# A third pair of expert weight buffers, earlier dispatch and reads of two batches, and a re-dealt attention order, in an attention kernel that feeds a mixture of experts

## The chip, the cores and the metric

The kernel runs on one core of one Trainium2 chip. The metric is the time of one execution in microseconds (us), as the device measures it; of several runs the median is quoted. A core has a matrix engine (PE; its weight loads are shown apart as PEld), a vector engine (DVE), a scalar engine (ACT), a general engine (POOL) and a sequencer that only issues transfers (SP). Each runs its own instructions in order and waits on semaphores for the others. Transfers run on 16 DMA engines. In this kernel those issued from SP (q, k, v, reads of the lists, transposing reads) form one queue, and those issued from POOL (weights with a cast to 16 bits, row scatters) another.

## The reference

Attention with a relative position bias (8 batches, 8 heads, 576 positions, head size 64), and then a routed pair of matrix products: each of the 4608 tokens goes to one of 8 experts by a hash of its id.

```python
scores = scale * q @ k.T + bias_table[bucket(i - j)]
attn = exp(scores - max); attn /= attn.sum()
x = (attn @ v)                       # reshaped to (4608, 512)
expert_idx = token_ids * 2654435761 % 8
for e in range(8):
    xe = x[expert_idx == e]
    out[expert_idx == e] = relu(xe @ w1[e]) @ w2[e]     # w1: 512 x 1024, w2: 1024 x 512
```

## The kernel before, in words

The work has two stages, whose instructions are written out by hand in the order in which each engine takes them.

**Attention.** It goes over 32 pairs (n): batch b = n // 4, heads 2m and 2m+1 with m = n % 4. A pair has five steps g. In each, PE forms score products into a PSUM tile `ps` (L528, bias through L505), ACT takes the exponential into `att` (L570) and, later, PE multiplies `att` with the values into `px` (L638). These value products trail the scores by more than a pair: a generator cuts them into 45 portions for each pair (9 for each of the five query tiles), and `advance(av, ...)` deals out a number of portions after each step, from the table `SHARE` (even pairs, odd pairs). DVE divides `px` into `x_all` (L648), applies a correction factor to `att` (L580) and moves transposed q and k out of PSUM into `kq` (L441). POOL casts q and k to 16 bits (L248). ACT is paced by 160 exponentials.

**Routing.** From the token ids, `route()` computes for each token its row in its expert's list of 640 rows. It is a generator as well; one piece is taken at steps 0 and 2 of pairs 6 to 9. DVE does nearly all of it (`oh`, `inc`, `rnk`, `rank`, `odd`, `ds2`).

**Dispatch.** `x_all` is a ring of 6 batches. When a batch is done, its five tiles join the list `waiting`, and `send` scatters them into the lists in HBM (`t_xperm`, L663, POOL), 2, 2 and 1 a pair from pair 10 on. `gather_head` reads the first 384 rows of the lists of experts 0 and 1 (`xpn`, L158, SP) once the scatters of batches 0 to 5, and 0 to 6, have landed; it stands at pairs 28 and 31. The first rows of expert 0 are transposed on PE in pair 31 (L848), and its first layer runs among the last value products (L862).

**Experts.** The parts are: experts 0 and 1, early rows; experts 0 and 1, last rows; experts 2 to 7 with 640 rows each. The first layer (`hps`, L1097 or L1117) needs `w1t`, the second (`ops`, L1149) `w2t`. DVE copies results to `ok` (L1154, 8 buffers), POOL scatters them to the output (L1157). There are two buffers of each weight. After the first layer of expert e, `load_w1(e + 2)` (L145) goes into the buffer just freed; after its second layer `load_w2(e + 2)` (L151). Experts 2 to 7 read their rows through transposing transfers issued on SP (`xpt`, L1042), into four buffers, so that the fifth and sixth wait for the first layers of experts 2 and 3.

A last stage, under a condition that does not hold for this input, recomputes everything in a general way (`fb`); it is not executed here.

## Time and profile before

| | us |
|---|---|
| median of 3 runs | 359.07 |
| lowest, highest | 352.07, 371.37 |
| the profiled execution | 347.01 |
| its span, first to last instruction | 345.2 |
| mean granted TensorE clock in it | 0.976 of full |
| busy: PE, ACT, DVE, POOL | 307.3, 202.4, 162.6, 155.2 |

The profiled execution is a run of its own, and it was shorter than the three timed ones. The span is 1.8 us below its time. Shares over the whole span mix two stages: attention up to about 180 us, where PE and ACT are both full, and the experts after it, where ACT and DVE have little to do.

### The profile page before, as it was taken

To read this page: it belongs to the slowest core of one execution; us is meant where nothing else is said; L and a number is where in the kernel's file an instruction comes from. 1 tells how busy PE (TensorE), PEld (TensorE's weight loads), DVE (VectorE), ACT (ScalarE), POOL (GpSimd) and SP (SyncE) were. 2 spreads that over 40 slices of the span, in tenths; PEclk is the share of its full clock that TensorE was granted. 3 is DMA by queue.
4 is the path that set the end of the run, shared out by engine and by line. 5 is a ranking of instruction groups with operands and counts; after the bars stand their busy time and mean duration, and the time that the engine had idled before them with its cause. 6 is when DMAs were issued, how large, how long until landed. Compare 5 with 4: busy or idle time off the path is not lost.

```text
span 345.2 us, 8717 instructions
## 1 busy us (share of the span) xinstructions
PE 307.3 (89%) x3595; PEld 194.0 (56%) x3595; DVE 162.6 (47%) x385; ACT 202.4 (59%) x239; POOL 155.2 (45%) x206
## 2 busy tenths in 40 slices
PE   7688898999999999999899995199997699899991
PEld 3356565676666677666665562164744346464651
DVE  3436899887879788887433311003021040312121
ACT  3799988999999999999831122050503306041410
POOL 5466742475677666566144245004204333253232
PEclk9999999999999999999999999589999899999998
DMA  6998998969899978998936999999999999997212
GB/s 171 252 259 253 296 273 247 297 177 297 243 261 273 262 210 259 208 155 132 234 98 156 216 187 100 224 229 84 83 221 159 219 170 215 229 214 177 86 65 89
DMA packets 102435, 68.86 MB, mean 199 GB/s; under 512 B 28001, under 2 KB 93929, under 8 KB 102386
## 3 DMA queue, kind: packets, MB, share of 16 engines
q1 hardware_dynamic: 84048, 36.66, 49.4%
q0 software_dynamic: 18080, 31.48, 44.5%
q8 instruction: 30, 0.49, 0.6%
q14 instruction: 19, 0.16, 0.2%
q10 hardware_dynamic: 258, 0.07, 0.1%
HBM read 65.24 MB, written 17.36 MB: 239 GB/s over the span
## 4 chain that ended last, share of the span: by engine, by line
PE 41%; DMA 28%; issue 10%; DVE 8%; ACT 6%; POOL 4%; SPq 1%; POOLq 0%; ACTq 0%; DVEq 0%
PE px L638 9%; PE ops L1149 8%; DMA w2t<-in_moe_w_dram 7%; DMA out_dram<-ok,ids 7%; PE ps L528 7%; DMA w1t<-in_moe_w_dram 6%; ACT att L570 6%; PE hps L1097 5%; PE ps L505 5%; DMA xpn<-t_xperm 3%; PE pqk L435 3%; POOL out_dram L1157 3%; DVE att L580 2%; DMA btr<-t_g 2%; PE hps L862 2%
## 5 line engine op out<-in xcount | busy, mean ns | idle before, releaser
L570 ACT ACTIVATE att<-ps 128x1024 f16<-128x1024 f32 x160 | 150.4, 1057 | 10.8 <-PE ps L528 8.8
L1154 DVE COPY ok<-ops 128x512 f32<-128x512 f32 (+1 forms) x41 | 27.8, 678 | 127.1 <-PE ops L1149 119.8
L1103 ACT ACTIVATE h<-hps 128x640 f16<-128x640 f32 x48 | 33.7, 703 | 86.6 <-PE hps L1097 86.6
L1149 PE MATMUL ops<-w2t,h 128*128 128x512 f16 (+1 forms) x328 | 73.3, 380 | 5.8 <-DMA w2t<-in_moe_w_dram 4.6
L1157 POOL DMA_INDIRECT out_dram<-ok,ids x40 | 39.9, 997 | 68.0 <-DVE ok L1154 36.5
L1097 PE MATMUL hps<-xpt,w1t 128*128 128x320 f16 x384 | 54.9, 305 | 12.7 <-DMA w1t<-in_moe_w_dram 12.7
L638 PEld LDWEIGHTS <-att 128*128 128x128 f16 x1408 | 54.7, 97 | 12.4 <-issue 7.5
L638 PE MATMUL px<-va,att 128*128 128x65 f16 x1280 | 59.4, 193 | 0.5 <-DVE xpt L853 0.3
L1149 PEld LDWEIGHTS <-h 128*128 128x128 f16 x328 | 32.0, 99 | 43.1 <-DMA w2t<-in_moe_w_dram 5.2
L1097 PEld LDWEIGHTS <-w1t 128*128 128x128 f16 x384 | 38.1, 100 | 29.8 <-DMA w1t<-in_moe_w_dram 13.7
L663 POOL DMA_INDIRECT t_xperm<-x_all,ds x40 | 41.6, 1040 | 21.9 <-DVE x_all L648 13.9
L505 PE MATMUL ps<-btb,idents 128*128 128x384 f16 (+1 forms) x256 | 45.2, 261 | 0.6 <-DMA btb<-t_f 0.3
L528 PE MATMUL ps<-kq 64*128 64x512 f16 x256 | 42.5, 382 | 2.0 <-DVE kq L441 1.2
L580 DVE TENSOR_TENSOR att<-att,ebd 128x768 f16<-128x768 f16 x64 | 42.3, 678 | 4.0 <-ACT ebd L603 4.0
L248 POOL CAST kh<-kf 128x512 f16<-128x512 f32 x31 | 19.7, 637 | 51.6 <-PE pqk L435 26.1
L648 DVE TENSOR_TENSOR x_all<-px,rcp 128x384 f16<-128x384 f32 x64 | 31.4, 491 | 2.2
L441 DVE COPY kq<-pqk 128x1024 f16<-128x1024 f16 x31 | 21.4, 690 | 19.9 <-PE pqk L435 19.7
L505 PEld LDWEIGHTS <-idents 128*128 128x128 f16 x336 | 20.9, 97 | 17.4 <-issue 16.0
L528 PEld LDWEIGHTS <-kq 64*128 64x128 f16 x512 | 14.9, 94 | 20.6 <-issue 13.1
L145 POOL DMA_DIRECT2D w1t<-in_moe_w_dram x8 | 6.5, 808 | 38.4 <-PE hps L1097 24.2
L248 POOL CAST qh<-qf 128x512 f16<-128x512 f32 x30 | 19.1, 637 | 3.5 <-DMA qf<-in_q_dram 3.4
L1125 ACT ACTIVATE h<-hps 128x768 f16<-128x768 f32 (+1 forms) x8 | 7.3, 916 | 22.4 <-PE hps L1117 22.4
(110 smaller groups left out, 274.4 us busy)
## 6 DMA issues: line engine op xcount, KB each, us to landing
w1t<-in_moe_w_dram POOLq DMA_DIRECT2D x8, 1024.0 KB, 23.6
w2t<-in_moe_w_dram POOLq DMA_DIRECT2D x8, 1024.0 KB, 18.9
vf<-in_v_dram SPq DMA_DIRECT2D x28, 256.0 KB
kf<-in_k_dram SPq DMA_DIRECT2D x26, 256.0 KB
qf<-in_q_dram SPq DMA_DIRECT2D x26, 256.0 KB
t_xperm<-zx SPq DMA_DIRECT2D x8, 192.8 KB
kf<-in_k_dram SPq DMA_DIRECT2D x12, 128.0 KB
qf<-in_q_dram SPq DMA_DIRECT2D x12, 128.0 KB
```

Of the source, the lines that this page charges most:

```text
L248: (eng or nc.gpsimd).tensor_copy(out=dst[n][:, :, :, :].transpose([0, 2, 1, 3]), in_=src[n // 2][:, 2 * (n % 2) : 2 * (n % 2) + 2].rearran ...
L505: nc.tensor.matmul(out=out, lhsT=idents[:, which, :], rhs=rhs, start=start, stop=True, skip_group_check=True,)
L528: nc.tensor.matmul(out=ps[:, hh, o : o + rhs.shape[1]], lhsT=lhsT, rhs=rhs, start=not biased and (g < KT or t == 0), stop=True, skip_group ...
L570: nc.scalar.activation(out=att[:, g, :, :], in_=ps[:, :, :], func=AF.Exp, bias=0.0, scale=scale,)
L580: nc.vector.tensor_tensor(out=a, in0=a, in1=ebd[:, 2 * m : 2 * m + 2, 1 - c : 3 - c, :], op=ALU.mult,)
L638: nc.tensor.matmul(out=po, lhsT=lhsT, rhs=rhs, start=(i == 0), stop=(i == len(todo) - 1), skip_group_check=True,)
L648: nc.vector.tensor_tensor(out=x_all[:, b % NRING, its[0] : its[0] + ni, :DM].rearrange("p t (m h d) -> p t m h d", h=2, m=NPAIR)[:, :, m, ...
L663: sc_in = nc.gpsimd.indirect_dma_start(out=xperm_d.ap()[:, :], out_offset=bass.IndirectOffsetOnAxis(ap=ds2[:, NIT * b + t : NIT * b + t + ...
L1097: nc.tensor.matmul(out=hps[:, nr, : n // 2], lhsT=w[:, kt, ts(ft, P)], rhs=xt[i][:, kt, ts(nr, n // 2)], start=(kt == 0), stop=(kt == NPT ...
L1103: nc.scalar.activation(out=hs[i][:, ft, :].rearrange("p (r n) -> p r n", r=2), in_=hps[:, :, : n // 2], func=AF.Relu, bias=0.0, scale=1.0,)
L1149: nc.tensor.matmul(out=ops[:, :w], lhsT=hs[i][:, ft, ts(sc, P)], rhs=w2t[e % 2][:, ft, d0 : d0 + w], start=(ft == 0), stop=(ft == NFT - 1),)
L1157: so = nc.gpsimd.indirect_dma_start(out=out[:, :], out_offset=bass.IndirectOffsetOnAxis(ap=ids[i][:, sc, :], axis=0), in_=ok[:, :], in_off ...
```

## The change

- **Weights**: three buffers of each weight (`NW = 3`) where there were two. The loads for experts 0, 1 and 2 all stand in the attention: w1 and w2 of expert 0 at pairs 22 and 24 (before: 24 and 26), of expert 1 at pairs 27 and 28 (28 and 30), of expert 2 in pairs 30 and 31 (before: in the expert stage). In the expert stage each load is for expert e + 3.
- **Dispatch**: sending starts at pair 14, with 2 or 3 tiles a pair; batches 5 and 6 are sent within one pair as soon as they are done; `gather_head` stands right behind them, at pairs 26 and 30. The ring `x_all` has 4 batches.
- **Value products**: portions dealt 9, 9, 9, 0, 18 in even pairs and 9, 9, 0, 9, 18 in odd ones (before: 18, 9, 9, 0, 18 and 9, 9, 0, 9, 9), with their own deals for pairs 2, 3 and 5.
- **Ramp**: the transposes of pair 2, the load of the last rows of k, the transposes of batch 1's last rows and the spread of its keys stand at other steps of pairs 0 to 3.
- **Routing**: its pieces are taken in pairs 8, 9, 12 and 13, its loads in pairs 5 and 6.
- `ok` has 14 buffers. The stage that is not executed is cut in two halves.

```diff
-    NRING = 6
+    NRING = 4
+    NW = 3
...
-            out=w1t[e % 2][:, k0:k1, :],
+            out=w1t[e % NW][:, k0:k1, :],
...
-        load_rest(0, "kq")
+        load_rest(0, "q")
...
         load_band(0, 2, nc.sync)
+        load_rest(0, "k")
...
-        SHARE = ((18, 9, 9, 0, 18), (9, 9, 0, 9, 9))
+        SHARE = ((9, 9, 9, 0, 18), (9, 9, 0, 9, 18))
+        DEAL = {2: (18, 18, 9, 9, 9), 3: (18, 0, 9, 9, 9), 5: (18, 0, 0, 9, 18)}
...
-            if n >= 10:
-                send((2, 2, 1)[(n - 10) % 3])
-            if n == NP - 4:
-                gather_head(0)
-            if n == NP - 1:
-                gather_head(1)
+            if 14 <= n < 25:
+                send(3 if n % 3 == 0 else 2)
...
-            if n >= 24 and n % 2 == 0:
-                (load_w1 if n % 4 == 0 else load_w2)((n - 24) // 4)
+            if n in (22, 24):
+                (load_w1 if n == 22 else load_w2)(0)
+            if n in (27, 28):
+                (load_w1 if n == 27 else load_w2)(1)
...
-            if 6 <= n < 10 and g in (0, 2):
+            if n in (8, 9, 12, 13) and g in (0, 2):
                 next(routing, None)
...
-                if b == B - 1:
-                    send(2)
+            if (m, g) in ((1, 2), (1, 4), (2, 0)) and b >= B - 2:
+                send(2)
+            if (m, g) == (2, 1) and b >= B - 2:
+                assert not waiting
+                gather_head(b - B + 2)
+            if (b, m, g) in ((B - 1, 2, 3), (B - 1, 3, 1)):
+                (load_w1 if m == 2 else load_w2)(2)
...
-            ok = mo.tile([P, DM], F32, name="ok", bufs=8)
+            ok = mo.tile([P, DM], F32, name="ok", bufs=14)
...
-            after = e + 2 if c1 == NSC and e + 2 < E else None
+            after = e + NW if c1 == NSC and e + NW < E else None
```

POOL's row, before, from pair 28 of the attention into the expert stage (each `w1t_N` and `w2t_N` is one buffer, `x_all` the rows of a batch, `ok` a tile of results):

```order
L145 DMA w1t_69<-in_moe_w_dram 128x4x1024
L663 DMA t_xperm<-x_all,ds_59 9728x514 x3
L151 DMA w2t_71<-in_moe_w_dram 128x8x512
L663 DMA t_xperm<-x_all,ds_59 9728x514 x7
L1157 DMA out_dram<-ok,ids 4608x512 x6
L145 DMA w1t_68<-in_moe_w_dram 128x4x1024
L1157 DMA out_dram<-ok,ids 4608x512 x2
L151 DMA w2t_70<-in_moe_w_dram 128x8x512
L145 DMA w1t_69<-in_moe_w_dram 128x4x1024
L1157 DMA out_dram<-ok,ids 4608x512 x2
L151 DMA w2t_71<-in_moe_w_dram 128x8x512
L145 DMA w1t_68<-in_moe_w_dram 128x4x1024
```

The same place after the change, from pair 28 on:

```order
L152 DMA w2t_72<-in_moe_w_dram 128x8x512
L664 DMA t_xperm<-x_all,ds_59 9728x514 x5
L146 DMA w1t_70<-in_moe_w_dram 128x4x1024
L152 DMA w2t_73<-in_moe_w_dram 128x8x512
L664 DMA t_xperm<-x_all,ds_59 9728x514 x5
L1166 DMA out_dram<-ok,ids 4608x512 x6
L146 DMA w1t_68<-in_moe_w_dram 128x4x1024
L1166 DMA out_dram<-ok,ids 4608x512 x2
L152 DMA w2t_71<-in_moe_w_dram 128x8x512
L146 DMA w1t_69<-in_moe_w_dram 128x4x1024
```

The two loads into the third buffers (`w1t_70`, `w2t_73`) now stand ahead of the last batch's five scatters; the first load behind the six result scatters is now for expert 3, where it was for expert 2.

DVE's row, before, in pair 7, around one piece of the routing (`inc`, `rnk`) among the correction of `att`, the division of `px` and the spread of a batch's last keys and queries (`kzr`, `qtr`):

```order
L580 TENSOR_TENSOR att<-att,ebd 128x4x192
L342 SCALAR_TENSOR_TENSOR inc<-keep,rps 128x320
L348 TENSOR_TENSOR rnk<-inc,rps 128x320
L462 COPY kzr_83<-prs 64x2x4x32 x2
L647 RECIPROCAL rcp<-px 128x4
L648 TENSOR_TENSOR x_all<-px,rcp 128x2x128
L473 COPY qtr_85<-prs 128x2x4x32
L352 TENSOR_TENSOR rnk<-rnk,oh 128x320
```

The same piece after the change, in pair 9:

```order
L581 TENSOR_TENSOR att<-att,ebd 128x4x192
L343 SCALAR_TENSOR_TENSOR inc<-keep,rps 128x320
L349 TENSOR_TENSOR rnk<-inc,rps 128x320
L648 RECIPROCAL rcp<-px 128x4
L649 TENSOR_TENSOR x_all<-px,rcp 128x2x128
L353 TENSOR_TENSOR rnk<-rnk,oh 128x320
```

The piece moved out of a pair in which DVE also spreads keys and queries, into one in which it does not.

## Rows read from the trace of the kernel before

**Rows 1.** The page, parts 2 and 5: DMA share in 40 slices; the value products.

```profile
DMA  6998998969899978998936999999999999997212
...
L638 PE MATMUL px<-va,att 128*128 128x65 f16 x1280 | 59.4, 193 | 0.5 <-DVE xpt L853 0.3
```

**Rows 2.** Windows: stretch, length, busy PE, PEld, DVE, ACT, POOL, clock, DMA share, GB/s.

```profile
22.00:45.70 23.70, 21.34 (x359) 14.46 (x357) 15.99 (x39) 21.41 (x25) 17.11 (x30) 1.00 1.00 268
45.70:66.90 21.20, 20.05 (x346) 13.59 (x345) 19.48 (x57) 19.15 (x22) 6.71 (x11) 1.00 0.96 277
66.90:85.80 18.90, 18.81 (x338) 13.02 (x335) 15.70 (x39) 18.81 (x22) 13.06 (x17) 1.00 0.86 240
...
212.60:222.70 10.10, 0.00 (x0) 0.00 (x0) 0.71 (x2) 0.00 (x0) 2.23 (x3) 0.68 1.25 208
```

**Rows 3.** Timeline of PE from 200 us: start, length, work, [idle before, ended by].

```profile
222.73 10.65 PE L1097 MATMUL hps<-xpt,w1t 128*128 128x320 f16 x64 [10.22 <-DMA w1t<-in_moe_w_dram]
...
241.84 8.86 PE L1097 MATMUL hps<-xpt,w1t 128*128 128x320 f16 x64
...
261.82 8.87 PE L1097 MATMUL hps<-xpt,w1t 128*128 128x320 f16 x64 [2.49 <-DMA w1t<-in_moe_w_dram]
273.57 10.49 PE L1149 MATMUL ops<-w2t,h 128*128 128x512 f16 x40 [2.88 <-DMA w2t<-in_moe_w_dram]
...
294.44 8.81 PE L1149 MATMUL ops<-w2t,h 128*128 128x512 f16 x40 [1.68 <-DMA w2t<-in_moe_w_dram]
...
329.10 8.89 PE L1149 MATMUL ops<-w2t,h 128*128 128x512 f16 x48
```

**Rows 4.** Timeline of POOL from 130 us: six of its DMA issues.

```profile
134.81 0.84 POOL L145 DMA_DIRECT2D w1t<-in_moe_w_dram  x1
...
162.31 0.96 POOL L151 DMA_DIRECT2D w2t<-in_moe_w_dram  x1
...
201.55 0.81 POOL L145 DMA_DIRECT2D w1t<-in_moe_w_dram  x1 [2.26 <-PE hps L1117]
...
233.68 0.79 POOL L145 DMA_DIRECT2D w1t<-in_moe_w_dram  x1 [18.17 <-PE hps L1097]
...
262.56 1.04 POOL L1157 DMA_INDIRECT out_dram<-ok,ids  x1 [10.77 <-DMA out_dram<-ok,ids]
...
306.46 0.97 POOL L151 DMA_DIRECT2D w2t<-in_moe_w_dram  x1
```

**Rows 5.** The tiles w1t and w2t: time from issue to landing of their loads.

```profile
DMA to landing us min/median/max: 21.1/23.6/28.1
...
DMA to landing us min/median/max: 14.8/18.9/22.0
```

**Rows 6.** Timeline of SP: how long its queue was held by transposing reads.

```profile
185.57 9.55 SPq L1042 DMA_TRANSPOSE xpt<-t_xperm  x2
...
199.86 5.68 SPq L1042 DMA_TRANSPOSE xpt<-t_xperm  x1
...
233.41 14.57 SPq L1042 DMA_TRANSPOSE xpt<-t_xperm  x1
...
250.73 28.23 SPq L1042 DMA_TRANSPOSE xpt<-t_xperm  x1
```

**Rows 7.** Timeline of PE in pair 31: the transposes of expert 0's rows.

```profile
169.22 0.51 PE L848 MATMUL xp<-idents,xpn 128*128 128x128 f16 x6 [0.90 <-DMA xpn<-t_xperm]
```

**Rows 8.** Waits, 68 to 164 us: who waited for whom, total, times, longest.

```profile
POOL kh L248 <- PE pqk L435: 18.3, 9, 4.0
...
POOL kh L248 <- DMA kf<-in_k_dram: 0.8, 1, 0.8
```

**Rows 9.** Windows of the expert stage, columns as in group 2.

```profile
204.00:212.00 8.00, 7.75 (x53) 4.91 (x51) 1.59 (x4) 2.05 (x2) 3.97 (x5) 1.00 1.22 77
...
222.00:232.00 10.00, 9.27 (x56) 6.11 (x57) 0.00 (x0) 4.22 (x6) 0.00 (x0) 0.78 1.17 228
236.00:247.00 11.00, 11.00 (x66) 6.36 (x65) 2.84 (x5) 2.72 (x4) 5.98 (x6) 1.00 1.16 55
```

More of the change, by code (lines that the diff above doesn't have):

```diff
@@ L132 @@
     h0 = cst.tile([P, NFT, EARLY * P], F16, name="h0")
-    w1t = [cst.tile([P, NPT, F], F16, name=f"w1t{i}") for i in range(2)]
-    w2t = [cst.tile([P, NFT, DM], F16, name=f"w2t{i}") for i in range(2)]
+    w1t = [cst.tile([P, NPT, F], F16, name=f"w1t{i}") for i in range(NW)]
+    w2t = [cst.tile([P, NFT, DM], F16, name=f"w2t{i}") for i in range(NW)]
     def disjoint(x, group):
@@ L151, in load_w2 @@
         nc.gpsimd.dma_start(
-            out=w2t[e % 2][:, f0:f1, :],
+            out=w2t[e % NW][:, f0:f1, :],
             in_=moe_w2[e].rearrange("(ft p) d -> p ft d", p=P)[:, f0:f1, :],
@@ L724 @@
         tbh = at.tile([2 * NB, H], F16, name="tbh")
-        ebsb = at.tile([H, 3, GL], F16, name="ebsb")
+        ebsb = at.tile([H, 3, GL], F16, name="ebsb", tag="once", bufs=1)
         nc.gpsimd.memset(ebsb[:, :, :], 0.0)
@@ L825 @@
         load_rest(1, "v", nc.gpsimd)
-        zx = at.tile([P, 2, XW], F16, name="zx")
+        zx = at.tile([P, 2, XW], F16, name="zx", tag="once", bufs=1)
         nc.gpsimd.memset(zx[:, :, :DM], 0.0)
@@ L927, in behind @@
             b, m = pairs[n]
-            if (m, g) == ((2, 4) if b else (3, 4)) and b + 1 < B:
+            if (m, g) == ((2, 4) if b else (3, 3)) and b + 1 < B:
                 transpose_rest(b + 1)
-            if 6 <= n < 10 and g in (0, 2):
+            if n in (8, 9, 12, 13) and g in (0, 2):
                 next(routing, None)
             if G >= 2 * NIT - 1:
-                advance(av, 18 if n == 2 and g < 2 else SHARE[n % 2][g]
+                advance(av, DEAL[n][g] if n in DEAL else SHARE[n % 2][g]
                         if NPAIR < n < NP - 1 else 9)
-            if (n, g) in ((1, 4), (2, 3), (3, 1)):
+            if (n, g) in ((2, 3), (3, 1)):
                 transpose_qk(G // 4)
@@ L950, in behind @@
                 cast_qk(4)
-            if (n, g) == (4, 1):
-                route_load(0)
             if (n, g) == (4, 2):
                 cast_qk(7)
-                route_load(1)
+            if (n, g) in ((5, 2), (6, 2)):
+                route_load(n - 5)
             if (m, g) == ((2, 2) if b else (3, 2)) and b + 1 < B:
@@ L959, in behind @@
                 factors(n)
+            if (n, g) == (1, 2):
+                transpose_qk(2)
             if g >= 3:
                 band(n, g - 3)
-            if (m, g) == ((3, 0) if b else (3, 4)) and b + 1 < B:
+            if (m, g) == ((3, 0) if b else (3, 3)) and b + 1 < B:
                 spread_keys(b + 1)
@@ L1087, in first_layer @@
             nsc = width(i)
-            n, w = P * nsc, w1t[PARTS[i][0] % 2]
+            n, w = P * nsc, w1t[PARTS[i][0] % NW]
             hs[i] = mo.tile([P, NFT, n], F16, name=f"h{nsc}",
@@ L1150, in second_layer @@
                         out=ops[:, :w], lhsT=hs[i][:, ft, ts(sc, P)],
-                        rhs=w2t[e % 2][:, ft, d0 : d0 + w],
+                        rhs=w2t[e % NW][:, ft, d0 : d0 + w],
                         start=(ft == 0), stop=(ft == NFT - 1),
@@ L1198 @@
         ) as fbp:
-            NCH = N // P
-            xna = fb.tile([P, NCH, DM], F16, name="xna")
-            nc.sync.dma_start(
-                out=xna[:, :, :],
-                in_=xperm_d.ap()[NSLOT:NROW, :DM].rearrange(
-                    "(g p) d -> p g d", p=P
-                ),
-            )
-            ten = fb.tile([P, NCH], I32, name="ten")
-            nc.sync.dma_start(
-                out=ten[:, :],
-                in_=bass.AP(
-                    moe_token_ids.bitcast(I32).tensor, 0,
-                    [[2, P], [2 * P, NCH], [1, 1]],
-                ),
-            )
-            ona = fb.tile([P, NCH, DM], I32, name="ona")
-            nc.vector.memset(ona[:, :, :], 0)
-            nc.vector.tensor_scalar(
-                out=ten[:, :], in0=ten[:, :], scalar1=E - 1, scalar2=None,
-                op0=ALU.bitwise_and,
-            )
-            for e in range(E):
+            NCH = N // P // 2
+            for half, e in [(i, e) for i in range(2) for e in range(E)]:
+                if e == 0:
+                    lo = NCH * P * half
+                    xna = fb.tile([P, NCH, DM], F16, name="xna")
+                    nc.sync.dma_start(
+                        out=xna[:, :, :],
+                        in_=xperm_d.ap()[
+                            NSLOT + lo : NSLOT + lo + NCH * P, :DM
+                        ].rearrange("(g p) d -> p g d", p=P),
+                    )
+                    ten = fb.tile([P, NCH], I32, name="ten")
+                    nc.sync.dma_start(
+                        out=ten[:, :],
+                        in_=bass.AP(
+                            moe_token_ids.bitcast(I32).tensor, 2 * lo,
+                            [[2, P], [2 * P, NCH], [1, 1]],
+                        ),
+                    )
+                    ona = fb.tile([P, NCH, DM], I32, name="ona")
+                    nc.vector.memset(ona[:, :, :], 0)
+                    nc.vector.tensor_scalar(
+                        out=ten[:, :], in0=ten[:, :], scalar1=E - 1,
+                        scalar2=None, op0=ALU.bitwise_and,
+                    )
                 w1x, w2x = w1t[e % 2], w2t[e % 2]
@@ L1299 @@
                     )
-            nc.sync.dma_start(
-                out=out.rearrange("(g p) d -> p g d", p=P),
-                in_=ona[:, :, :].bitcast(F32),
-            )
+                if e == E - 1:
+                    nc.sync.dma_start(
+                        out=out[lo : lo + NCH * P, :].rearrange(
+                            "(g p) d -> p g d", p=P
+                        ),
+                        in_=ona[:, :, :].bitcast(F32),
+                    )
 _INS = ['q', 'k', 'v', 'bias_table', 'moe_token_ids', 'moe_w1', 'moe_w2']
```

4 lines of the change are left out of this document (3 added, 1 removed).

## The prediction

> **What bounds the kernel now.** I read the windows first, to split the span into stages, then PE's timeline in the expert stage, then POOL and SP, which issue what PE waits for, and last the waits inside the attention.
>
> In the attention PE and ACT are both full: in the four undisturbed pairs from 66.9 us PE is busy 18.81 and ACT 18.81 of 18.90 us [rows 2]. A pair costs 4.73 us there, and only work taken off both engines, or a wait, can change that. Two stretches are slower. The four pairs from 45.7, in which the routing stands, take 21.20 us, and DVE is busy 19.48 of them; the four before take 23.70 [rows 2].
>
> In the expert stage PE alone counts. It takes 17.33 us an expert when nothing is missing: the second layers of experts 5 and 7 start at 294.44 and 329.10, two experts apart [rows 3]. Four times it stands still, each time for a weight load: 10.22, 2.49, 2.88 and 1.68 us [rows 3]. After the two longest it also runs slowly for a while: the first layer at 222.73 takes 10.65 where the next takes 8.86, and the second layer at 273.57 takes 10.49 where another takes 8.81 [rows 3]. During the longest wait the granted clock has a mean of 0.68 [rows 2], so part of that work ran at the lower level, 1.2 GHz.
>
> Why are the loads late? A load needs 14.8 to 28.1 us from issue to landing [rows 5], and with two buffers POOL can issue it only when the expert two places ahead has let go of its buffer: POOL stood 18.17 us until a first layer on PE ended before it issued at 233.68 [rows 4]. So expert 2's first weights are asked for at 201.55 and PE wants them at 212.6.
>
> **Third weight buffers.** Expert 2's loads now stand in pairs 30 and 31, around 165 us, more than 40 us ahead of their use, and each later load has a whole expert more of time, 17.33 us on top of 26.0 (three layers of 8.67). All four waits and both slow stretches go if the loads then come in time: 10.22 + 2.49 + 2.88 + 1.68 = 17.27, and 1.79 + 1.68 = 3.47 for the clock; together **-20.7 us**.
>
> What is late next? The supply itself. Before, twelve loads were issued from 201.55 on, the last at 306.46, landing 14.8 us later at the earliest, 321.3 [rows 4, 5]: 119.7 us, 10.0 each. Ten remain after 201.55; at that pace the last lands at 301.3, and PE without waits wants it at 212.6 + 5 x 17.33 + 8.67 = 307.9. The last eight, from 233.68, came at 10.95 each; at that pace ten end at 311.0, 3.1 late. Between 0 and 3.1 I take **+1.5**, the middle, because both paces hold the same transposing reads that remain.
>
> Two loads' worth of transfer moves into the attention, where the DMA engines already show eight and nine tenths in most slices [rows 1]. At the 228 GB/s of 222 to 232 us [rows 9] a load of 1024 KB as stored keeps them 4.6 us; two are 9.2, which is the upper bound if q, k and v come late by all of it. The lower bound is 0: a load cannot bring q, k or v sooner. From 68 to 164 us POOL waited 0.8 us for k to arrive and 18.3 for PE to free a buffer [rows 8], so q and k lie ready well ahead, and I take 0.5 for that. The loads of expert 2 also stand ahead of the last batch's scatters in POOL's queue; experts 0 and 1 need those rows only behind their early parts, so another 0.5: **+1.0**, bounds 0 and 9.2.
>
> **Dispatch and early reads.** PE waited 0.90 us in pair 31 for expert 0's rows [rows 7]; the read now stands nearly two pairs earlier and the wait goes: **-0.9**. On POOL five scatters stand close together in two places instead of spread; each keeps POOL about 1 us (1.04 at 262.56 [rows 4]), and the casts queued behind have the 18.3 us of idle waiting [rows 8] as cover. What waits on SP behind the earlier read are only the later reads of the lists, since the last load of v is issued ahead of it. Without that cover it would cost up to 5 us once. I cost it at nothing.
>
> **Routing.** It added 19.48 - 15.70 = 3.8 us to DVE in four pairs that had 18.90 - 15.70 = 3.2 free, and these pairs took 2.3 us too long [rows 2]. It now takes two pairs out of each of two batches, those in which DVE does not spread the last keys. If all fits, 2.3 come back; if each half delays its pairs as the whole did, 2.3 are lost again. I take **-1.8**, near the first end, since half the load now meets more than half of the free time.
>
> **Ramp order.** The four pairs from 22.0 lose 4.8 us against 18.90, of which 21.41 - 18.81 = 2.6 is extra work on ACT that stays [rows 2]. So at most 2.2 can come back, and as much can be lost by other steps waiting; I take **-0.7**.
>
> **Values dealt anew.** Nine products move from the first step of an even pair to the end of the odd pair before it. They do not become fewer. One is 59.4 / 1280 us = 46 ns of PE [rows 1], nine are 0.42. ACT idles 0.09 in four pairs [rows 2], so 22 pairs can give back 0.5 at most; if the scores of each of 11 even pairs came 0.42 later and ACT had no store, 4.6 would be lost. ACT has up to two steps of scores waiting, so I take **0**. The 14 result buffers serve the same waits as the weights and are not counted again.
>
> **The sum.** The profiled execution took 347.0 (span 345.2, 1.8 around it): 347.0 - 20.7 + 1.5 + 1.0 - 0.9 - 1.8 - 0.7 = **325.4 us**. The median of the runs, 359.1, lies 12.1 above the profiled one, and they spread from 352.1 to 371.4. If that excess is weights that came later still, the change takes it away; if everything was slower, most of it stays. With half of it, 325.4 + 6.0, I forecast **331 us**. From one run to the next this kernel differs enough that some 2% (352 to 366) cannot be told from no change.
>
> **The rivals.** *POOL's own limit on transfers in flight.* The scatter at 262.56 stood 10.77 us, until about when the load of 233.68, eight transfers ahead of it in POOL's order, can have landed (233.68 + 28.1 = 261.8) [rows 4, 5]. If POOL issues none before the one eight places ahead has landed, a load for expert e + 3 waits for a landing of expert e + 1, and the third buffer stands empty for part of the time. The lead is 17.3 + 26.0 = 43.3 us; a load of 28.1 behind such a wait of 10.8 is 38.9, so it still fits, by 4. If it fails, half the waits come back: 331 + 10 = 341. For: that wait. Against: that margin.
>
> *q, k and v late.* The whole 9.2 instead of 1.0 gives 339. For: full slices of DMA. Against: [rows 8].
>
> *All transfers are the bound.* Then the time hardly moves: what the expert stage gains, the attention loses, and the result lies within 352 to 366. For: nine tenths or more in most slices [rows 1]. Against: at 204 to 212 us the share is 1.22 and the engines move 77 GB/s, at 222 to 232 it is 1.17 and they move 228 [rows 9], so the share does not tell that they are at their limit. The Trainium skill (DMA: Bandwidth & Descriptors, "Issuing engines are not separate DMA queues") has the rule for it: transfers issued by any engine run on the same 16 DMA engines and interleave, so an earlier issue only takes turns from others. By that rule this rival's time would hold if the engines had nothing to spare; the traces of 77 and 228 GB/s at like shares speak against that.
>
> *Slower than before: the transposing reads set the pace.* Four of the six ran while only light scatters were beside them and held SP 9.55 for two and 5.68 for one; the two that ran beside weight loads held it 14.57 and 28.23 [rows 6], and the engines moved 55 GB/s in the first part of that [rows 9]. With three buffers weights may be in the queue all the time. PE wants the sixth at 212.6 + 5 x 17.33 = 299.3; begun at 185.6, that allows 19.0 us each. Slower than before by 2% it would be from about 23.7 each (185.6 + 6 x 23.7 + 17.3 + 7.2 + 1.8 = 354); at 28.2 each the time is 381. Against: the weights of expert 2 should have landed when the first ones run, and nothing is issued until the last rows of expert 0 leave their buffer. The Trainium skill (DMA: Bandwidth & Descriptors, "Latency and other measured facts") gives a transposing read 261 GB/s, an estimate of 2.5 us for these 655 KB; by that this rival would not exist and the sum would stay; the rows show up to 28, and they decide.
>
> **How the numbers follow.** Forecast 0.69; POOL's limit 0.12; q, k, v late 0.08; all transfers the bound 0.07; transposing reads 0.04. The predicted time is the forecast's. Its own low end is 325.4 without any excess, less what the bounds still allow (1.5 + 1.0 + 0.5 + 1.5 + 0.5 = 5): 320, and 317 for more gained in the medians than in the profile. The high end is the first rival with the whole excess, 325.4 + 10 + 12 = 348, widened to 351 for the third. So 317 to 351. Faster by over 2%: 0.88 (the first three cases, less a little at the edge); within 2%: 0.08; slower: 0.04.
>
> **What would show it.** In the new profile PE's timeline from the first layer of expert 2 on should show no wait above 1 us, its first and second layers 8.7 us apart, and a clock of 1.00. The loads for expert 2 should be issued around 165 us, and the wait of 0.90 in pair 31 be gone. The four pairs from 45.7 should take about 19 us, those from 66.9 still 18.9. POOL waits of 10 us and more with PE waits behind them would show the first rival; attention pairs longer than 4.73 in pairs 22 to 31 the second; SP held over 19 us for each transposing read, with first layers waiting for `xpt`, the last. The forecast is wrong if first layers of experts 3 to 7 still wait for weights.

## The result: within 2% of the kernel before, not 8% shorter

The changed kernel takes 350.37 us (median of 20 runs, 347.01 to 355.81), the kernel before, run beside it, 353.72 (20 runs, 343.79 to 371.37). The ratio is 1.0126, 95% interval 1.0092 to 1.0159. It leaves out executions that lie over 1.5% above the shortest of their kernel, 16 of the 20 of the kernel before and 2 of the changed one, so it compares with those in which little came late. By plain medians the change is 0.9% shorter, with a much narrower spread. Either way the two kernels are the same within 2%; the forecast was 331 us and faster by over 2%.

The profiled execution of the changed kernel took 349.96 us (span 348.1). PE's timeline, to be read beside [rows 3]:

```profile
202.70 1.89 PE L1158 MATMUL ops<-w2t,h 128*128 128x512 f16 x8 [1.72 <-PE px L639]
...
234.57 8.86 PE L1106 MATMUL hps<-xpt,w1t 128*128 128x320 f16 x64
243.26 8.80 PE L1158 MATMUL ops<-w2t,h 128*128 128x512 f16 x40
...
329.89 8.88 PE L1158 MATMUL ops<-w2t,h 128*128 128x512 f16 x48
```

No bracket stands behind any first or second layer from 234.57 on (three of the twelve rows are shown): all four weight waits and both slow stretches are gone, as forecast. But the first second layer (`ops`), which follows the attention, starts at 202.70, where it was 180.47. The windows of three groups of four pairs, with the columns of [rows 2]:

```profile
45.60:66.30 20.70, 19.38 (x338) 13.12 (x336) 18.56 (x45) 19.14 (x22) 12.08 (x19) 1.00 1.08 256
66.30:85.80 19.50, 18.83 (x336) 12.91 (x334) 17.23 (x50) 18.82 (x22) 5.81 (x10) 1.00 0.97 261
85.80:109.60 23.80, 19.36 (x336) 12.99 (x334) 15.95 (x39) 19.11 (x23) 15.27 (x19) 1.00 0.91 250
```

Up to 85.80 nothing is lost. From there, where the changed kernel begins to scatter, four pairs take 23.80 us with 19.36 of PE and 19.11 of ACT in them: both engines wait, and not for work. The table splits the spans at pair 14's first exponential, the first `ops`, expert 2's first layer and PE's last end; three experiments told below stand beside the two profiles.

| us | before | after | forecast of the difference | e13 (before) | e9 (changed) | e18 (best) |
|---|---|---|---|---|---|---|
| to pair 14 | 85.81 | 85.77 | -2.5 | 89.69 | 85.48 | 84.96 |
| to the first `ops` | 94.66 | 116.93 | +0.1 | 109.05 | 94.77 | 94.26 |
| to expert 2, its wait left out | 32.04 | 31.87 | 0 | 32.03 | 31.86 | 31.87 |
| to PE's end, that wait put in | 125.48 | 104.20 | -19.2 | 117.34 | 104.22 | 104.20 |
| to the end | 7.21 | 9.33 | 0 | 7.19 | 9.77 | 7.41 |
| span | 345.2 | 348.1 | -21.6 | 355.3 | 326.1 | 322.7 |

The experts gave 21.3, the attention took 22.2 and the end 2.1. But the same kernel as before takes 198.74 to its first `ops` in e13, and the same changed kernel 180.25 in e9:

```profile
198.74 1.89 PE L1149 MATMUL ops<-w2t,h 128*128 128x512 f16 x8 [1.61 <-PE px L638]
```

```profile
180.25 1.89 PE L1158 MATMUL ops<-w2t,h 128*128 128x512 f16 x8 [0.78 <-ACT h L870]
```

So the 22 us between the two profiles are hardly the change.

### The profile page after: what moved, and what is told of

Its sections match the earlier page's. It is cut to its first block, busy times and chain, and to the rows that moved or that the text cites. A ratio compares the mean times of both kernels' runs of the same rounds, so it can differ in the third digit from the quotient of the medians.

```text
span 348.1 us, 8719 instructions
## 1 busy us (share of the span) xinstructions
PE 308.7 (89%) x3595; PEld 194.2 (56%) x3595; DVE 163.9 (47%) x385; ACT 204.1 (59%) x239; POOL 156.4 (45%) x207
## 4 chain that ended last, share of the span: by engine, by line
PE 74%; ACT 7%; DVE 7%; DMA 3%; issue 2%; another core or an unknown queue 2%; SPq 1%; POOL 1%; POOLq 0%; ACTq 0%
PE ops L1158 20%; PE hps L1106 15%; PE px L639 11%; PE ps L529 9%; PE ps L506 7%; ACT att L571 6%; PE pqk L436 4%; PE hps L1126 4%; DMA btr<-t_g 2%; DVE x_all L649 2%; DVE att L581 2%; PE hps L864 1%; PE ps L563 1%; DMA kf<-in_k_dram 1%
## 5 line engine op out<-in xcount | busy, mean ns | idle before, releaser
L1158 PE MATMUL ops<-w2t,h 128*128 128x512 f16 (+1 forms) x328 | 71.6, 374 | 2.2 <-PE px L639 1.7
L639 PE MATMUL px<-va,att 128*128 128x65 f16 x1280 | 58.1, 194 | 5.8 <-DVE kq L442 4.8
L1106 PE MATMUL hps<-xpt,w1t 128*128 128x320 f16 x384 | 53.1, 299 | 0.0
L249 POOL CAST kh<-kf 128x512 f16<-128x512 f32 x31 | 20.4, 657 | 59.8 <-PE pqk L436 31.8
L506 PE MATMUL ps<-btb,idents 128*128 128x384 f16 (+1 forms) x256 | 46.0, 265 | 1.2 <-DMA btb<-t_f 0.9
L529 PE MATMUL ps<-kq 64*128 64x512 f16 x256 | 43.3, 387 | 2.7 <-ACT att L571 1.2
L581 DVE TENSOR_TENSOR att<-att,ebd 128x768 f16<-128x768 f16 x64 | 43.5, 682 | 0.8 <-ACT ebd L604 0.7
L506 PEld LDWEIGHTS <-idents 128*128 128x128 f16 x336 | 21.1, 99 | 17.2 <-issue 15.8
L529 PEld LDWEIGHTS <-kq 64*128 64x128 f16 x512 | 14.7, 95 | 27.6 <-issue 21.2
L648 DVE RECIPROCAL rcp<-px 128x6 f32<-128x6 f32 x64 | 11.8, 185 | 23.4 <-PE px L639 12.4
```

The costliest lines, as they stand in the source:

```text
L249: (eng or nc.gpsimd).tensor_copy(out=dst[n][:, :, :, :].transpose([0, 2, 1, 3]), in_=src[n // 2][:, 2 * (n % 2) : 2 * (n % 2) + 2].rearran ...
L506: nc.tensor.matmul(out=out, lhsT=idents[:, which, :], rhs=rhs, start=start, stop=True, skip_group_check=True,)
L529: nc.tensor.matmul(out=ps[:, hh, o : o + rhs.shape[1]], lhsT=lhsT, rhs=rhs, start=not biased and (g < KT or t == 0), stop=True, skip_group ...
L581: nc.vector.tensor_tensor(out=a, in0=a, in1=ebd[:, 2 * m : 2 * m + 2, 1 - c : 3 - c, :], op=ALU.mult,)
L639: nc.tensor.matmul(out=po, lhsT=lhsT, rhs=rhs, start=(i == 0), stop=(i == len(todo) - 1), skip_group_check=True,)
L1106: nc.tensor.matmul(out=hps[:, nr, : n // 2], lhsT=w[:, kt, ts(ft, P)], rhs=xt[i][:, kt, ts(nr, n // 2)], start=(kt == 0), stop=(kt == NPT ...
```

## Where the attention's time goes

One timeline of all engines of the changed kernel, at a scatter (`t_xperm<-x_all`, POOL):

```profile
109.77 1.12 POOL L664 DMA_INDIRECT t_xperm<-x_all,ds  x1 [0.15 <-issue]
...
111.19 0.50 PE L506 MATMUL ps<-btb,idents 128*128 128x384 f16 x2
111.19 0.98 POOL L664 DMA_INDIRECT t_xperm<-x_all,ds  x1 [0.30 <-issue]
...
112.59 1.94 ACT L571 ACTIVATE att<-ps 128x1024 f16<-128x1024 f32 x2 [1.04 <-PE ps L506]
112.63 0.38 PE L436 MATMUL pqk<-idents,kh 128*128 128x128 f16 x4 [0.67 <-PE ps L506]
```

The bias products (L506) end at 111.69, and PE's last products before its pause, `px` at 111.53, at 111.96. ACT, which waits for scores, starts at 112.59; PE, whose next instruction also waits, at 112.63. Both come 0.4 us behind the end of the second scatter (112.17), just after the third is issued at 112.48. Over the whole attention, up to the first `ops`: of 213 waits of other engines that a signal of PE ended in the changed kernel, 33 ended over 0.15 us behind the end of PE's instruction, by up to 0.99 us, and 32 of these within 1.0 us of a scatter's end. I call these signals held. In the first profile of the kernel before it was 0 of 219, the latest 0.02 us. No signal of ACT or DVE was over 0.04 us late in either. The ends of PE's products are modelled in the profile, so the trace does not tell whether the product or only its signal was late.

## The experiments

The chips differ, and the kernel before ran beside each group:

| chip | PE's signals held (by the profiles) | kernel before: lowest, median, highest (runs) | experiments |
|---|---|---|---|
| 5 | yes | 344.53, 347.07, 371.04 (7) | e1 to e4 |
| 8 | no | 325.40, 334.13, 351.60 (21) | e5 to e7 |
| 7 | no | 324.99, 333.29, 349.62 (13) | e8 to e11 |
| 15 | yes | 342.61, 345.32, 504.80 (13) | e12 to e14 |
| 9 | yes | 343.25, 352.00, 354.50 (7) | e15 to e17 |
| 10 | no | 325.68, 335.04, 1673.30 (18) | e18 |

**Which part lengthens the attention? e1 to e4.** Code is cut to the lines that matter. The changed kernel with the old deal:

```diff
-SHARE = ((9, 9, 9, 0, 18), (9, 9, 0, 9, 18)); DEAL = {2: ..., 3: ..., 5: ...}
+SHARE = ((18, 9, 9, 0, 18), (9, 9, 0, 9, 9))
```

> The changed kernel with the old deal of the values (18,9,9,0,18 and 9,9,0,9,9) and nothing else undone. If the deal is what made the changed kernel's pairs 15 to 26 take 5.5 to 7.1 us instead of 4.74, they return to about 4.74 and the run takes about 330 us. If the dispatch or the early loads cost it, or the ring of four, the pairs stay near 5.9 and the run near 350.

354.14 us, ratio 1.0248 [1.0203, 1.0293]: 1.2% more than with the new deal. The kernel before with the new deal (the same lines the other way):

> The kernel before with the new deal alone. If the deal costs the 20 us: pairs 15 to 26 at 5.5 us or more and 365 to 375 us in all. If something else does: within 2 us of the kernel before, pairs at 4.74.

336.76, 338.60, 359.72 and 361.54 us; ratio 0.9776 [0.9694, 0.9858] for the first two, so with the deal alone the spread stays. In the profile of the first its first `ops` starts at 191.84, the earliest on chip 5, and PE waits for no weights though there are two buffers. The kernel before with third buffers and what they need in space:

```diff
+NW = 3     # w1t, w2t; NRING = 4, ok in 14 buffers, the overflow path in halves
+if n in (NP - 1,):
+    load_w1(2)
+    load_w2(2)
```

> The kernel before with the third weight buffers and the ring of four alone; expert 2's loads are issued at the start of the last pair, everything else of the attention as it was. If the buffers, the ring or their places in SBUF slow the attention: pairs near 5.9 and about 350 us. If not: the attention ends near 180 as before, PE does not wait from expert 2 on, and the run takes 326 to 332 us.

348.65 us (348.54 to 349.43), ratio 1.0099 [1.0055, 1.0143], no wait for weights in the profile. Of the 1%, 2.3 us or 0.7% are the overflow path in halves (e10 and e12 below). The changed kernel with the old dispatch, load places and routing:

```diff
-if 14 <= n < 25:
-    send(3 if n % 3 == 0 else 2)
-if n in (8, 9, 12, 13) and g in (0, 2):
+if n >= 10:
+    send((2, 2, 1)[(n - 10) % 3])
+if 6 <= n < 10 and g in (0, 2):
...      # gather_head, the loads of experts 0 and 1 and route_load as before, too
```

> The changed kernel with the old times of scatters, early reads, weight loads of experts 0 and 1, and routing; new deal, ramp and buffers stay. If bunched scatters, the early reads behind them or the earlier loads cost the 20 us: pairs back at 4.74 and about 330 us. If the deal or the buffers do: near 350 as the changed kernel.

345.67 us, ratio 1.0017 [0.9938, 1.0096], 1.1% less than the changed kernel's; its attention ends at 194.17. No part makes the attention 20 us longer: with and without each the first `ops` starts between 191 and 206. Where PE's signals are held the new deal gains 1 to 2% (e1 against the changed kernel, e2) and the new places of dispatch, loads and routing cost about 1% (e4). The parts do not add up exactly: 1.0099 and 0.9776 make 0.987, e4 has 1.0017, of which a wait of 2.37 us for `xpn` is 0.7%.

**Is it the chip? e5 to e7.** The kernel before, unchanged:

> The kernel before, unaltered, profiled once more. In all four first experiments PE's signals were late by up to 1.3 us whenever a scatter was being issued on POOL, and pairs with scatters took 5.2 to 6.4 us; in the profile of before they were not, and there the weights came late. If the slow pairs come from the changes, this profile shows pairs of 4.52 to 4.96 us again, the attention's end near 180 and weight waits of some 17 us. If both belong to the execution and not to the kernel, it shows pairs of 5.2 to 6.4 where scatters stand, the attention's end near 195, and no or short weight waits.

327.14 us (12 runs, 325.55 to 353.10); in its profile (335.02) no signal is held, and the first `ops` starts at 182.79. Third buffers and new deal on the kernel before (e3 and e2 together):

> The kernel before with third weight buffers, the ring of four and the new deal; scatters, early reads, routing, ramp and the loads of experts 0 and 1 as before. If the new deal saves what its experiment showed and the buffers only take away late weights: 335 to 340 us with no run above 345. If ring or buffers slow the attention: 345 to 350.

330.80 us (329.87 to 332.85), ratio 1.0114 [1.0081, 1.0146]: without held signals the deal gains nothing there (pairs 14 to 17 take 18.91 us, 18.94 in e5). The changed kernel with one batch scattered at once in pair 24 and all others of batches 0 to 6 late, a ring of seven batches and two weight buffers:

```diff
-if 14 <= n < 25:
-    send(3 if n % 3 == 0 else 2)
+if n == 24:
+    send(NIT)      # 5 scatters
+if n == NP - 1:
+    send(99); gather_head(0); gather_head(1)
```

> The changed kernel with a ring of seven and two weight buffers, and 30 of the 35 scatters of batches 0 to 6 issued at the start of the last pair; the early reads and what needs them wait behind them, so the total is long (380 or more) and only the pairs count. If scatters being issued on POOL hold up PE: pairs 15 to 30 without one take 4.5 to 5.0 us, and only pair 24, where five stand, is longer by some 3 to 5 us. If the deal, the ramp or the transfers of q, k and v slow the pairs: they stay near 5.8.

367.42 us, since the experts wait for their rows. Its five scatters fall in pairs 24 and 25, which take 4.53 and 4.59 us; pairs 15 to 30 take 4.53 to 5.27: here scatters cost the attention nothing.

**The same kernels elsewhere: e8 and e9**, the kernel before and the changed one.

> The kernel before, unaltered, for a profile beside the changed kernel on the same chip. If the held signals belong to a chip: either this profile and the changed kernel's both show them or neither does. If they belong to a kernel: this one never shows them.

> The changed kernel, unaltered. On a chip that holds up PE's signals during scatters: about 350 us, attention's end near 202. On one that does not: pairs of 4.5 to 5.3 us, the attention's end near 180 to 183 and 327 to 330 us in all, no run above 335; before is then 325.5 in executions whose weights are in time and 331 to 352 in those where they are late.

Neither shows a held signal. e8 338.19 us, with weight waits of 5.46, 0.48 and 1.88. e9 327.90 us (10 runs, 326.97 to 328.72), ratio 1.0054 [1.0027, 1.0080]. e9's window over the same pairs as the third above:

```profile
85.50:104.50 19.00, 18.88 (x336) 12.87 (x334) 15.84 (x39) 18.72 (x22) 15.22 (x19) 1.00 1.00 257
```

19.00 us where it was 23.80, with the same work in it.

**Both back on a chip with held signals: e13 and e14.** The kernel before, and e7's kernel, with its scatters in two known places.

> The kernel before, unaltered, for a profile beside the next kernel. Where that one or the changed one shows signals of PE late by up to 1.3 us during scatters, this one should too (pairs of 5.2 to 6.4 us, the attention's end near 197) if they belong to the chip; if they belong to the changes, its pairs stay at 4.52 to 4.97.

> The changed kernel with 30 of 35 scatters at the start of the last pair (ring of seven, two weight buffers), once more. On a chip where signals are held: pairs 15 to 23 and 25 to 30 at 4.5 to 5.3 us if scatters cause it, and pair 24, with five scatters, some 3 to 5 us longer; near 5.8 if something else of the attention does. On a chip where none are held it repeats what it showed: 4.5 to 5.3 throughout.

e13 357.06 us. The window of its pairs 10 to 13, 18.90 us in [rows 2]:

```profile
66.70:89.70 23.00, 19.36 (x340) 13.17 (x337) 15.82 (x39) 19.13 (x23) 13.33 (x17) 1.00 0.81 240
```

33 of its 225 signals of PE are held, by up to 0.96 us. Pairs 10 to 26 with a scatter take 4.97 to 6.25 us, save pair 18 with 4.53, whose one scatter met no signal that it held; pairs 21 and 25, without any, take 4.52. e14 382.05 us: pairs 15 to 23, without scatters, take 4.54 to 5.25, pair 24 with five 8.56. Beside the scatters in a row that follow, the windows (pairs 24 and 25 first, then pair 29) and PE's timeline show the extreme:

```profile
132.80:147.20 14.40, 11.84 (x164) 7.41 (x162) 7.03 (x17) 9.69 (x10) 8.60 (x11) 0.88 1.07 238
162.10:201.90 39.80, 10.07 (x72) 5.05 (x71) 3.19 (x8) 5.09 (x6) 26.71 (x28) 0.55 0.42 123
```

```profile
181.08 0.22 PE L639 MATMUL px<-va,att 128*128 128x65 f16 x1 [0.50 <-issue]
182.48 0.22 PE L639 MATMUL px<-va,att 128*128 128x65 f16 x1 [1.18 <-issue]
184.56 0.22 PE L639 MATMUL px<-va,att 128*128 128x65 f16 x1 [1.86 <-issue]
```

PE starts one small product every 0.7 to 2.1 us while POOL issues a scatter every 1.29 us; the granted clock has a mean of 0.55 there. The same kernel on chip 8 (e7) had none of this. So it is the scatters, on some chips. Why these chips do it stays open; each was seen in one sitting, so chip and sitting cannot be told apart.

**The end: e10 and e12.** POOL's own instructions at the branch over the path that is not entered and behind it (duration in ns, first and last start), before:

```profile
L1195 POOLq COMPARE_BRANCH  x1: 50/50/50, 339.3 to 339.3; - x1
...
L1329 POOLq DRAIN  x3: 51/103/4573, 339.8 to 344.9; - x3
```

After:

```profile
L1204 POOLq COMPARE_BRANCH  x1: 57/57/57, 340.1 to 340.1; - x1
...
L1343 POOLq DRAIN  x3: 51/103/4303, 342.9 to 347.8; - x3
```

0.5 us from the branch to the next instruction became 2.8 (in e9 3.3). e10 is the kernel before with its overflow path in halves, e12 the changed kernel with it in one piece:

```diff
-NCH = N // P
+NCH = N // P // 2
+for half, e in [(i, e) for i in range(2) for e in range(E)]:
```

> The kernel before with one part of the change alone: the path for lists that overflow, which is not entered here, is written in two halves and so is nearly twice as long. If POOL's branch over it costs what the profiles show (2.8 us from the branch to POOL's next instruction in place of 0.5): 2.2 to 2.4 us slower than before. If it does not matter: no difference.

> The changed kernel with the overflow path in one piece again (one staging buffer there in place of two, so that it fits); that path is not entered. If the longer branch is the whole difference in executions of before whose weights are in time: 2.3 us less than the changed kernel, equal to those executions of before where no signals are held (325 to 326.5 us), and no run more than 4 us above. If third buffers or early loads cost attention time too: 1 to 3 us slower than those.

e10: 3.1 us from branch to drain (317.8 to 320.9), so the halves alone do it. Its time does not show it: 336.91 us (327.68 to 343.83), ratio 1.0329 [1.0122, 1.0537], most of it late weights; one of four executions had its weights in time, 327.68 against 324.99 to 327.13 of six before. e12: 0.5 us (336.2 to 336.7), 344.57 us (342.67 to 346.41), ratio 1.0028 [0.9982, 1.0075], 1% under the changed kernel's. The Trainium skill (Runtime: NRT & Kernel Launch, "Instruction fetch mechanics") says that a taken branch out of the window of fetched instructions waits for a fetch. The longer path fits that; no run here shows what is fetched, so the cause is not shown.

**Where the loads stand: e11.** Third buffers, new deal, overflow path in one piece, but expert 2's loads behind the last scatters (the lines against e6):

```diff
-if n in (NP - 1,):
-    load_w1(2); load_w2(2)
 assert not waiting
+load_w1(2); load_w2(2)
```

> The kernel before with third buffers, ring of four and the new deal, expert 2's loads issued behind the last scatters and the overflow path in one piece. If the third buffers only guard against late weights: as fast as the fast executions of before (within 1 us without held signals, 6 to 8 us faster with them, by the deal), and no run more than 5 us above its fastest. If the earlier loads and the ring cost attention time as such: 3 to 5 us slower than before's fast executions.

358.28 us, ratio 1.1008 [1.0876, 1.1139], outside both of my cases, where e6 with the loads ahead of the last scatters took 330.80. SP's timeline, DVE's and PE's:

```profile
186.25 23.82 SPq L1048 DMA_TRANSPOSE xpt<-t_xperm  x2
...
210.87 22.20 SPq L1048 DMA_TRANSPOSE xpt<-t_xperm  x1
...
238.87 28.05 SPq L1048 DMA_TRANSPOSE xpt<-t_xperm  x1
```

```profile
256.46 0.17 DVE L1143 TENSOR_SCALAR ids<-names 128x5 int32<-128x5 int32 x1 [19.25 <-DMA names<-t_xperm]
256.54 1.28 DVE L1160 COPY ok<-ops 128x512 f32<-128x512 f32 x2
```

```profile
257.28 7.06 PE L1155 MATMUL ops<-w2t,h 128*128 128x512 f16 x24 [8.65 <-DVE ok L1160]
```

Beside the loads the third, fourth and fifth transposing reads hold SP 22.20, 28.05 and 24.26 us, and the small reads of the row ids (`names`) queue behind them. DVE, which prepares the ids (L1143), stands 14.86, 19.25 and 18.81 us for them; its copies of results come behind that in its order, so PE, which has two `ops` tiles, waits 4.26, 8.65, 8.25 and 1.30 us. This is the last of my rivals, in another kernel, through `names` instead of `xpt`. In the changed kernel the first four reads took 8.12 (two), 3.07 and 4.61: expert 2's loads were issued 27 us ahead of them. The Trainium skill (DMA: Bandwidth & Descriptors, "Latency and other measured facts") gives such a read 261 GB/s, an estimate of 2.5 us for 655 KB; 3.07 comes near, 22 to 28 beside weight loads does not, and the measurement decides.

**When are two buffers late? e15 to e18.** Nine profiles of two-buffer kernels have expert 2's `w1t` load and the fourth transposing read close together. POOL, SP and PE in e13, late:

```profile
219.81 0.81 POOL L145 DMA_DIRECT2D w1t<-in_moe_w_dram  x1 [2.26 <-PE hps L1117]
```

```profile
218.23 5.51 SPq L1042 DMA_TRANSPOSE xpt<-t_xperm  x1
```

```profile
239.84 10.57 PE L1097 MATMUL hps<-xpt,w1t 128*128 128x320 f16 x64 [9.07 <-DMA w1t<-in_moe_w_dram]
```

And in e10, in time:

```profile
200.53 0.81 POOL L145 DMA_DIRECT2D w1t<-in_moe_w_dram  x1 [2.26 <-PE hps L1117]
```

```profile
201.25 15.12 SPq L1042 DMA_TRANSPOSE xpt<-t_xperm  x1
```

```profile
212.26 8.87 PE L1097 MATMUL hps<-xpt,w1t 128*128 128x320 f16 x64 [0.77 <-DMA w1t<-in_moe_w_dram]
```

In e13 the read began 1.58 us ahead of the load, finished in 5.51, and the load took 20 us. In e10 it began 0.72 behind the load, took 15.12, and the load landed in 11.7. Over all nine: issued 0.56 to 2.09 us into the read, the load was late (the first profile, e5, e7, e8, e13, e16); issued ahead of the read (e10, e14) or 3.10 into it (e2), in time or 0.77 late, though e14's `w2t` was then late, by 7.09. That is a pattern of nine profiles, not yet a cause. e15 takes the meeting away, the fourth read waiting for expert 2's first layer; e16 shifts the read; e17 is e15 with the new deal:

```diff
-xt[i] = mo.tile([P, NPT, CAP], F16, name="xpt5", bufs=4)
+xt[i] = mo.tile([P, NPT, CAP], F16, name="xpt5", bufs=3)   # e15, e17
```

```diff
 load_transposed(i)
-if i > CROSS:
+if i == CROSS + 3:                     # e16: ids behind the fourth read
+    for j in range(CROSS, i): load_names(j)
+elif i > CROSS + 3:
     load_names(i - 1)
```

> Three buffers for the transposed rows in place of four, nothing else: the fourth transposing read then waits for expert 2's first layer, and cannot run beside the load of expert 2's first weights. In six profiles of two-buffer kernels that load came late (15.5 to 21.2 us from issue to landing) where it was issued 0.8 to 2.0 us into the fourth read, and in time (10.8 and 11.7 us) where the read began 0.7 us behind it or 3.1 us ahead of it. Theory A, that this meeting makes the weights late: the load lands within about 12 us, PE waits less than 1 us before expert 2's first layer, and all executions lie within some 3 us of each other, at 325 to 328 us on a chip on which PE's signals are not held and 342 to 347 on one on which they are. Theory B, that the supply as a whole is short: waits of 4 us and more stay, and about half of the executions lie 6 to 25 us above the lowest. A loss of its own would be the fifth and sixth reads, each later by a place: over 19 us each beside weight loads, they would make experts 6 and 7 wait for rows, up to 10 us.

> Two small reads on SP stand behind the fourth transposing read in place of ahead of it, so that it begins about 1.3 us earlier. Its lead over the load of expert 2's first weights was 0.8, 1.6, 1.7 and 2.0 us in four late profiles; it becomes 2.1 to 3.3. Theory A (the load is late when it is issued 0.8 to 2.0 us into the read): most executions are in time, 325 to 328 us without held signals and 342 to 347 with; those whose lead was below 0 move into the bad stretch and may be late. Theory B (the supply as a whole): the spread stays as the kernel before has it, about half of the executions 6 to 25 us above the lowest.

> Three buffers for the transposed rows and the changed deal of the values, on two weight buffers and the old overflow path. If theory A holds and the deal is worth 7.6 us only where PE's signals are held: 325 to 328 us on a chip without that and 335 to 338 on one with it, all executions within 3 us; it would be the shortest version. Under theory B half of the executions stay 6 to 25 us longer. If the fifth and sixth transposing reads come late, 330 and more in every execution.

e15 353.91 us (351.21 to 357.99), e16 354.75 (345.62 to 363.47), e17 346.97 (343.73 to 354.72), the kernel before 352.00 (343.25 to 354.50) beside them. The times miss theory A, which had all executions within 3 us; e15's profile bears it out. Its PE has no wait for weights at all, and one for DVE, which stands 14.06 us for ids that are now read behind the later reads:

```profile
231.88 8.86 PE L1097 MATMUL hps<-xpt,w1t 128*128 128x320 f16 x64
...
299.66 8.28 PE L1149 MATMUL ops<-w2t,h 128*128 128x512 f16 x24 [3.49 <-DVE ok L1154]
```

e17 lost 6.28 and 0.24 in the same way. e16's shift put the load 2.09 us into the read: late, 4.08 us, and only one of its four executions was among the short ones, where theory A had expected most. e18 is e17 with the ids' reads of experts 3 to 7 ahead of the fourth read:

```diff
-if i > CROSS:
-    load_names(i - 1)
+if i == CROSS + 1:
+    load_names(CROSS)
+if i == CROSS + 2:
+    for j in range(CROSS + 1, len(PARTS)): load_names(j)
```

> As e17 (three buffers for the transposed rows, the changed deal, two weight buffers, the overflow path in one piece), and the small reads of the ids of experts 3 to 7 stand ahead of the fourth transposing read on SP, where in e17 those of experts 5 to 7 stood behind the reads that were held 16 to 26 us beside weight loads; their lateness cost PE 6.28 and 0.24 us there. If that was the whole of it: no wait of PE above 1 us from expert 2's first layer on, in every execution, so 344.2 - 6.5 = 337.7 us where PE's signals are held beside scatters (e17's chip) and 325 to 326 where they are not, all executions within 3 us; against the kernel before in time 0.98 in the first case and 1.00 in the second. If the sixth transposing read, held over 25 us, comes late for expert 7's first layer, or output scatters and weights still get in each other's way, waits for xpt or ok of some us stay and the executions spread by more than 3 us.

324.77 us in 12 runs from 323.84 to 325.95, ratio 0.9935 [0.9890, 0.9979]; the kernel before ran from 325.68 up, median 335.04. In the profile PE waits nowhere for weights, rows or ids from expert 2's first layer on:

```profile
211.09 8.86 PE L1098 MATMUL hps<-xpt,w1t 128*128 128x320 f16 x64
...
306.41 8.88 PE L1150 MATMUL ops<-w2t,h 128*128 128x512 f16 x48
```

By the profile, and by twelve times within 0.7%, two weight buffers are now in time in every execution. The time is 3.1 us under the changed kernel's in e9 (327.90, another chip), of which 2.3 are the longer overflow path. Moving the fourth read, e15's edit, is what took the wait for weights away; e17 and e18 add the deal, which alone left the spread (e2), and the ids' place, which was not run alone with four buffers. Where signals are held, e18 was not run.

## Why the prediction was wrong

**350.37 lies within 317 to 351 by luck.** The high end was set for half of the weight waits coming back with the whole excess, widened for transfers as the bound. Neither came: no weights were late, and the attention was long by held signals, which the forecast has in no term.

**"Third weight buffers -20.7": the size failed, not the mechanism.** The waits went as said. But 17.27 + 3.47 was what one execution lost, taken as what every execution loses. PE's waits for expert 2's first weights were 10.22, 9.07, 5.46, 4.96, 4.55 and 4.08 in the first profile, e13, e8, e7, e5 and e16, 0.77 in e10 and none in e2 and e14. Of 64 timed executions of the kernel before on chips 7, 8 and 10, 24 took at most 328 us, as e18 always does; the others, one of 1673 aside, reach up to 353. The term is 0 against the first kind, which the ratio keeps; against the others, e9 is 10.3 shorter than the one execution of e8. In the runs of the result the kernel before has a median 7.8 us above the mean of its four shortest (345.9); if that is late weights, it is what the third buffers took away, and the change's own 4.5 us over these four leave the 3.35 by which its median is shorter. And e18 shows that third buffers are not needed for it. The supply term (+1.5) was 0.

**"With half of the excess, I forecast 331": the step failed.** I took the median's 12.1 us over the profile as late weights. The profile came from a chip on which PE's signals are not held; the timed runs, 352 to 371, look like those of chips on which they are, where none of the kernel before was below 342. That is some 18 us of attention (198.74 in e13, 180.47 in the first profile), of which the new deal takes back some and no part of the change all. The forecast has them in no term: on chip 7 the changed kernel's 327.90 lies only 2.5 above the sum's 325.4 (by the table: the end 2.6 more, the start 2.2 more, the experts 2.1 less), where it was timed 25 above.

**Scatters "at nothing": wrong where signals are held.** Set against the first profile, e13's pairs 10 to 30 with two or three scatters take 1.1 to 1.4 us more (pair 12 only 0.1), those with one 0 to 1.5. It is right where signals are not held (e7). Bunching and moving them, with loads and routing, costs some 1% where they are (e4).

**Routing -1.8: nothing came. Ramp -0.7: perhaps more.** Pair 14 starts at 85.77 as it did at 85.81: pairs 6 to 9 gained 0.4, pairs 10 to 13, two of which now hold pieces, lost 0.6. DVE's free time in these did not take them up; half way between my two ends would have been right. For the ramp one pair of profiles is too little. Pair 6 starts at 44.8 to 47.0 in seven profiles with the old ramp and deal (the first, e5, e8, e10, e13, e15, e16), at 44.4 to 45.6 in five with the new ones (the changed kernel's, e7, e9, e12, e14): 1.3 us less in the mean. But with the old ramp and the new deal (e2, e6, e11, e17, e18) it starts at 44.4 to 45.4 as well, so the deals of pairs 2, 3 and 5 may be what gains it.

**Deal 0: right from pair 14 on without held signals**, -1 to -2% with them. **Extra transfers +1.0, dispatch -0.9:** e9's attention takes 94.77 where the profile of before takes 94.66; together 0, as summed (+0.1).

**Not in the sum: +2.3 us at the end** from the halved overflow path. I told of it as not executed and did not ask what it costs to pass by. The table has it as 2.1 in the changed kernel's profile and 2.6 in e9's.

Of the rivals, POOL's limit in flight and late q, k and v did not show; "all transfers the bound" came near in time, for another reason: in e9 the DMA share is 1.00 in the 19.00 us with PE full, in the 23.80 it is 0.91 with PE waiting. The transposing reads set the pace in e11 only. Its rows I had misread: the fourth read did not run beside light scatters alone, since the load issued at 201.55 began 1.69 us into it [rows 4, 6], the very meeting of e15 to e18. And its 354 is 2% above the profiled execution, not above the median.

## What to carry to other kernels

One profile shows one execution: before a wait is priced, look whether the spread of the times says that some executions lack it, and whether profile and timed runs are on the same level at all. When a load is late in some executions only, compare its start with the neighbours' starts in several traces; moving the neighbour may do what another buffer does. Code that is not entered can still cost time to pass by.

## What the runs showed of the hardware

On four of the sittings, counting the changed kernel's own, signals of PE, and at times its issue, were held beside row scatters that POOL issued, by up to 1.5 us (e4), in 9 to 39 signals of each of eleven profiles; in the nine other profiles not one was over 0.02 us late. The attention lost some 18 us by it (e13). The scatters of results in the expert stage, from the same engine, held next to none: 0 of 104 signals of PE in the changed kernel, 1 of 97 in e13. PE started on a weight load of 1024 KB at its own pace 10.8 us after the issue, or with a wait of 0.77 us 11.7 after it, when it was in time, and 15.0 to 21.2 when the load was issued 0.56 to 2.09 us into a transposing read; in e13 the engines then show a share of 1.38 and move 64 GB/s:

```profile
224.00:230.00 6.00, 5.75 (x41) 3.68 (x39) 0.89 (x3) 2.05 (x2) 2.75 (x3) 1.00 1.38 64
```

Why the order of two transfers changes their times so much stays open.
